# Token blocks 0 and 1 of the last matrix product joined to the seven-product groups, and the second gate's weight blocks converted inside the first gate

## The chip, the cores and the metric

The kernel runs on one core of one Trainium2 chip. The metric is the device time of one execution in microseconds (us), lower being better. The kernel before takes 741.22 us (median of 3 runs, 740.75 to 741.38).

## What is computed

The reference is a layer of two mixers on 2048 tokens of 1024 numbers. First `h = x + A(layernorm(x))`, where `A` is attention in four segments of 512 tokens with a memory that is carried from segment to segment. Then

```python
z  = gelu(layernorm(h) @ w_in)            # 2048 x 3584
z1 = z[:, :1792]
z2 = layernorm(z[:, 1792:])
g  = w_sp @ z2 + b_sp[:, None]            # w_sp is 2048 x 2048: over tokens
out = h + (z1 * g) @ w_out                # w_out is 1792 x 1024
```

The change is in the last two lines, but for one instruction that it moves in the attention part.

## The kernel before

Each engine has its own list of instructions, written out in program order by the Python code, and runs it in order. A recorder (`record`, line 87) derives the semaphore waits from the bytes that instructions read and write. Nothing is scheduled automatically: where a line stands in the code is where its instruction stands in its engine's queue. All instructions are issued through one helper, so that the profile gives them all line 214; they are told apart by their tiles. SyncE (SP in the profile) issues the DMAs.

**Attention.** A loop over n = 0 to 31 (segment and group of heads). In each pass TensorE makes projections, scores, products with values and, from the second segment on, eight-matmul pieces of the output projection (`ps<-wo,oT`); ScalarE makes the exponentials; VectorE normalises (`rd`, `otok`, `rdm`, `tm`), adds the residual (`hch`) and does parts of the next stage in between. One of these is `w_half` (line 932), which scales a 128x3584 piece of w_in from bfloat16 to float16 in one VectorE instruction (`wih<-win,sc`). `w_half(0)` stands at the end of pass 26 (line 1081) and `w_half(2)` at the end of pass 28.

**The gate** (`gate`, line 1257) is the product with w_sp. It runs twice: `gate(0, ...)` (line 1602) for output tokens 0 to 1023 and `gate(1, ...)` (line 1733) for tokens 1024 to 2047. Each half of w_sp is four blocks, b11, b12, b22 and b21, and four differences of them, t1 to t4 (`SUMS`, line 1236: t1 = b12 - b11, t2 = b22 - t1, t3 = b22 - b12, t4 = b21 - t2). With these, and with sums `ss` of z2's blocks (`s_sum`), a two-by-two block product takes seven block products, not eight. A gate has seven groups g of 128 + 128 channels, and a group is seven products of eight 128x512 matmuls: t2, t1, b11 or b21, t3, b21, t4, b22. ScalarE puts the bias into a PSUM bank before the first product adds to it (`seed_a`, `seed_b`, `seed_c`), and copies a bank out in the middle of a group (`copy_u`); VectorE takes results out (`out`) with the factor z1. After each product of a group the gate calls `each(g, k)`, k = 0 to 3, which places extra work there; `seam` is called after the first three b11 products.

The second gate's blocks are transposed early by DMA and parked in DRAM (`w_spT`). `q_load` (line 1219) brings one block back, 1 MB, `q_conv` (line 1222) scales it into float16 on VectorE (`b11g<-b11q,sc`, 128x4096), and `q_sum` makes one difference (128x4096). The g in a name marks the second gate's blocks and the h the first gate's (`b11h`). `HOME1` (line 424) gives each block its place in SBUF, which sets what must be dead before it can be loaded.

**Between the gates** stand four plain units (`units`, `out_unit`, lines 1519 and 1379): token blocks 0 and 1, times the two 512-wide halves of w_out, each 14 bfloat16 matmuls 128x512 (`ps<-w_out,z1T`), 56 in all. While TensorE runs them, VectorE makes t1, converts b22 and b21, and starts t2; b22 and b21 are loaded at that time too.

**The last product** is y = z1 * g times w_out. It runs for pairs of token blocks: two blocks, two halves of the contraction (seven chunks of 128 each) and two halves of the output make a two-by-two block product, and seven products of seven float16 matmuls do it (`NG = 7` groups, line 1672; `tcs` says which blocks; the loop at line 1770). These take y in float16 with a scale: the second gate writes it so (`z1x`); the first gate's results (`z1T`, bfloat16) are squared and summed on ScalarE (`y0_norm`) and converted on VectorE (`y0_conv`) during the second gate. VectorE also makes the sums of w_out's blocks (`ob_sum`) and of y's (`y_sum`) there.

Of the kernel before, what the change touches and what calls it, by code (L numbers as in the profile page):

```python
# [13 lines left out]
D = 1024  # L14
# [248 lines left out]
def bass_sequential_preLN__memory_aug_infini_attn__mixer_gmlp__prompt_kernel(  # L263
# [156 lines left out]
    WO1 = [tens("w_out1%d" % i, [128, 7, 512], BF16, o * K) for i, o in enumerate((14, 22))]  # L420
    WO0H = [tens("w_out0h%d" % i, [128, 7, 512], F16, o * K) for i, o in enumerate((54, 198))]
    STG = [tens("stg%d" % i, [128, 8, 128], BF16, o * K) for i, o in enumerate((54, 56, 58, 198, 200, 202))]
    WSPT = nc.dram_tensor("w_spT", (4, 128, 4, 1024), BF16, kind="Internal").ap()
    HOME1 = {"b11": 4, "b12": 118, "b22": 46, "b21": 126, "t1": 38, "t2": 22, "t3": 118, "t4": 14}
    RAW1 = {k: tens(k + "q", [128, 4, 8, 128], BF16, HOME1[k] * K) for k in ("b11", "b12", "b22", "b21")}
    BH1 = {k: tens(k + "g", [128, 4, 8, 128], F16, o * K) for k, o in HOME1.items()}
    SQ0 = tens("sq0", [128, 14], F32, 928)
# [3 lines left out]
    FIN2 = [tens("fin2%d" % i, [128, 2, 2, 512], BF16, o * K) for i, o in enumerate((4, 8, 22, 26))]  # L431
    OT4 = [[tens("ot%d%d" % (i, k), [128, 512], F32, (o + 2 * k) * K) for k in range(4)] for i, o in enumerate((38, 118))]
    SY = [tens("sy%d" % i, [128, 4, 7, 128], F16, o * K) for i, o in enumerate((14, 126))]
    FIN = [tens("fin%d" % i, [128, 512], BF16, o * K) for i, o in enumerate((21, 29, 13, 12))]

    PS = nc.alloc_psum_tensor("ps", [128, 8, 512], F32)
    R.space[PS[:, 0, :].tensor.name] = ("psum", 0)
# [12 lines left out]
    def next_bank(hold=False):  # L450
        if free:
            b = free.pop(0)
            if not hold:
                free.append(b)
            return b
        b = rot["banks"][rot["n"] % len(rot["banks"])]
        rot["n"] += 1
        return b

    def mm8(dst, lhs, rhs, n=8):  # L460
        for i in range(n):
            pe.matmul(dst, lhs(i), rhs(i), start=(i == 0), stop=(i == n - 1))
# [529 lines left out]
    for n in range(LAST + 1):  # L992
# [224 lines left out]
        sp.dma_start(WSPT[n // 4, :, n % 4, :], STG[n % 6][:].rearrange("p c n -> p (c n)"))  # L1217

    def q_load(k):
        sp.dma_start(RAW1[k][:].rearrange("p j c n -> p j (c n)"), WSPT[Q4.index(k)])  # L1220

    def q_conv(k):
        dve.tensor_single_scalar(BH1[k][:], RAW1[k][:], SC[0][:], ALU.mult)

    def q_sum(o):
        a, b = SUMS[o]
# [30 lines left out]
    def gate(pr, perm, seam=lambda: None, mid=lambda: None, each=lambda g, k: None):  # L1257
# [32 lines left out]
        def seed_a(g):  # L1290
            act.activation(bank(ba(g)), BROW[0][:], ACTF.Copy, scale=RINV[:])
# [10 lines left out]
        def p1(g):  # L1302
            prod(ba(g), a_blk(0, 0, g), "b11")
# [16 lines left out]
        for g in range(7):  # L1320
# [50 lines left out]
    fins = {}

    def fin_load(u, q=sp):
        tc, lo, w = u
        k = len(fins) % 4
        fins[u] = FIN[k]
        q.dma_start(FIN[k][:, 0:w], out2d[tc * 128:(tc + 1) * 128, lo:lo + w])

    def out_unit(u, wsl, q=sp):
        tc, lo, w = u  # L1380
        b = next_bank()
        mm8(PS[:, b, 0:w], lambda i: Z1T[:, i, tc * 128:(tc + 1) * 128], wsl, n=14)
        fin = fins[u]
        dve.tensor_tensor(fin[:, 0:w], fin[:, 0:w], PS[:, b, 0:w], ALU.add)
        q.dma_start(out2d[tc * 128:(tc + 1) * 128, lo:lo + w], fin[:, 0:w])
# [130 lines left out]

    w0_load(1)

    units = [(tc, 512 * h, 512) for h in range(2) for tc in range(2)]

    def seam():
        sp_half("b21")
        for k in range(1, 4):
# [19 lines left out]
    def total(n, src, o=TOT):  # L1543
        pool.tensor_copy(SQB[:, 0:n], src[:])
        pe.matmul(PS[:, 7, 0:n], ONES[:], SQB[:, 0:n], start=True, stop=True)
        dve.tensor_reduce(out=o[:], in_=PS[:, 7, 0:n], axis=mybir.AxisListType.X, op=ALU.add)
        dve.tensor_single_scalar(o[:], o[:], 1e-30, ALU.max)
# [15 lines left out]
        t = 1024 + 512 * k  # L1563
        sp.dma_start(BROW[k][:], B_b_sp[t:t + 512].partition_broadcast(128))

    def w1_load(i):
        sp.dma_start(WO1[i][:], wout[:, 7 * i:7 * i + 7, 512:D])

    def each0(g, k):
        z1_norm(g, k)  # L1570
        for h, lo in ((1, 14), (0, 22)):
            for n in range(14):
                if 4 * g + k == lo + n // 3:
                    w_norm(h, n)
            if 4 * g + k == lo + 4 and h:
                w0_load(0)
        if (g, k) == (0, 0):
            pool.tensor_single_scalar(TW[:], TOT[:], float(2 * T * FH), ALU.mult)
        if (g, k) == (5, 1):
            w1_load(0)  # L1580
            fin_load(units[0])
        if (g, k) == (4, 3):
            total(28, SQY, TOTY)
        if (g, k) == (6, 0):
            brow_in(1)
            q_load("b11")
            q_load("b12")
        if (g, k) == (6, 1):
            fin_load(units[1])
            w1_load(1)  # L1590
        if (g, k) == (6, 2):
            brow_in(0)
            fin_load(units[2])
            fin_load(units[3])
            q_conv("b11")
        if (g, k) == (6, 3):
# [5 lines left out]
    gate(0, banks, seam, mid, each0)  # L1602
    q_load("b22")
    q_load("b21")

    def brow_sq():
        for k in range(2):
            act.activation(bank(7), BROW[k][:], ACTF.Square, scale=float(np.sqrt(2.0)), accum_out=BSQ[:, k:k + 1])
# [4 lines left out]
        power(YS)  # L1613
        dve.tensor_tensor(INVY[:], INV[0][:], YS[:], ALU.mult)

    brow_sq()
    pool.tensor_tensor(TOT[:], TOTY[:], TW[:], ALU.mult)
    rot["banks"], rot["n"] = [banks[k] for k in (1, 2, 4, 6)], 0
    free.clear()
    q_sum("t1")  # L1620
    for n, u in enumerate(units):
        out_unit(u, (lambda i: WO0[i // 7][:, i % 7, :]) if u[1] == 0 else
                 (lambda i: WO1[i // 7][:, i % 7, :]))
        if n == 0:
            s_sum(1, 0)
            s_sum(2, 0)
        if n == 2:
            scale_y()
            q_conv("b21")
        if n == 1:  # L1630
            q_conv("b22")
    q_sum("t2")
    s_sum(3, 0)
    q_sum("t3")
    q_sum("t4")

    OBG = {"b12": 0, "b22": 2, "t1": 1, "t2": 3, "t3": 4, "t4": 5}
    OBW = {"b11": 0, "b21": 1}
# [16 lines left out]
        dve.tensor_tensor(ob_c(o, *r), ob_c(a, *r), ob_c(b, *r), ALU.subtract)  # L1655

    def y0_scale():
        total(14, SQ0)
# [12 lines left out]

    NG = 7

    def tcs(g):
        return (2 + g, 5 + g) if g < 3 else (5 + g, 9 + g)

    def y_blk(i, j, g):
        t = 128 * tcs(g)[i]
        return Z1X[:, 7 * j:7 * j + 7, t:t + 128]

    def sy(k, g):
        if g == 0:
            return Z1X[:, 7 * (k // 3):7 * (k // 3) + 7, 128 * (1 - k % 2):128 * (1 - k % 2) + 128]
        return SY[g % 2][:, k - 1]

    def y_sum(k, g):
# [16 lines left out]
    def job(g, k, f, *a):  # L1703
        jobs.setdefault((g, k), []).append((f, a))

    for r in range(14):
        job(*divmod(1 + r // 2, 4), y0_norm, r)
    for h in range(4):
        job(2 + (h + 1) // 4, (h + 1) % 4, y0_conv, h)
        job(3 + (h + 1) // 4, (h + 1) % 4, y_sum, h + 1, 0)  # L1710
    job(2, 0, y0_scale)
    job(0, 0, scale_w)
    for r in range(7):
        job(1, 0, ob_load, "b12", r)
# [14 lines left out]
        for f, a in jobs.get((g, k), ()):  # L1729
            f(*a)  # L1730

    perm1 = [banks[k] for k in (0, 3, 5, 1, 2, 4, 6)]
    gate(1, perm1, each=each1)

    def o_prod(b, a, w, first, lo=0, hi=512):
        for i in range(7):
# [103 lines left out]
```

## Time and profile before

| what | value |
|---|---|
| time, median of 3 runs | 741.22 us (740.75 to 741.38) |
| the profiled execution's own time | 741.11 us |
| its span, first to last instruction | 739.5 us |
| TensorE clock granted | 1.00 |
| VectorE busy | 579.5 us, 78% of the span |
| ScalarE busy | 478.0 us, 65% |
| GpSimd busy | 267.0 us, 36% |
| first gate's last stage before the plain units | ends at 565.72 us |
| plain units | 565.72 to 577.80 us |
| second gate | 577.80 to 662.46 us |
| last product, seven groups | 662.46 us to the end |

Times in the trace are microseconds from the span's start. In a line of the timeline come the start, the duration of the piece, the engine, the operation, the tile written and the tiles read, the shape, and how many instructions the piece holds; in brackets stands the idle time of the engine just before, and what ended it. PE is TensorE, DVE VectorE, ACT ScalarE, POOL GpSimd. A TensorE piece's duration has the drain of its last matmul in it, so that the pitch of the matmuls is read from the distance of starts.

### The profile page before, as it was taken

The page shows a single profiled execution, that of the slowest core. Times are in us where ns is not written, and L with a number is a line of the kernel's source. Part 1 is how long each engine was busy: PE and PEld are TensorE (multiplying, and loading weights), DVE is VectorE, ACT ScalarE, POOL GpSimd, SP SyncE. Part 2 cuts the span into 40 slices and gives each one's busy share as a digit, 9 for nine tenths or more (in the row PEclk, how much of TensorE's full clock was granted, in tenths as well). Part 3 has the DMA queues.
Part 4 walks back from the last instruction along what each step waited for, and adds up shares of the span by engine and source line. Part 5 has one row for each costly group of instructions (what it writes and reads, how often), then busy time and mean ns, then how long its engine had stood idle before and what let it go on. Part 6 is the DMA issues. An engine that isn't in the chain of part 4 may idle for free.

```text
span 739.5 us, 13541 instructions
## 1 busy us (share of the span) xinstructions
PE 733.4 (99%) x5399; PEld 351.7 (48%) x5399; DVE 579.5 (78%) x1027; ACT 478.0 (65%) x684; POOL 267.0 (36%) x423
## 2 busy tenths in 40 slices
PE   8999999999999999999999999999999999999998
PEld 4444544544555445545554444444444444444444
DVE  5578889889988989878896777874556778866676
ACT  6777888888887888826886669966866282210000
POOL 2565555545554333110153899600000100005342
PEclk9999999999999999999999999999999999999999
DMA  9656568466645752654050036399539211031311
GB/s 302 176 172 149 114 149 180 126 155 161 172 101 165 250 178 59 169 131 129 29 142 1 1 58 128 60 198 188 168 123 329 68 44 35 1 114 64 107 58 57
DMA packets 148798, 92.64 MB, mean 125 GB/s; under 512 B 105984, under 2 KB 132864, under 8 KB 148224
## 3 DMA queue, kind: packets, MB, share of 16 engines
q1 hardware_dynamic: 147920, 91.00, 46.9%
q8 instruction: 42, 0.69, 0.4%
q10 hardware_dynamic: 816, 0.79, 0.3%
q14 instruction: 20, 0.16, 0.1%
HBM read 56.11 MB, written 12.58 MB: 93 GB/s over the span
## 4 chain that ended last, share of the span: by engine, by line
PE 96%; DVE 3%; DMA 1%; issue 0%; ACT 0%; DVEq 0%
PE ps L214 96%; DVE sq L214 1%; DMA wv<-in_A_wv_dram 1%; DVE hch L214 0%; DVE ps L214 0%; DVE otok L214 0%; DVE rd L214 0%; DVE wih L214 0%; DVE stats L214 0%; ACT L214 0%; DVE rdm L214 0%; DVE pqk L214 0%; DVE fin L214 0%; DVEq L224 0%; DVE tot L214 0%
## 5 line engine op out<-in xcount | busy, mean ns | idle before, releaser
L214 ACT ACTIVATE e<-ps 128x2048 bf16<-128x2048 f32 (+1 forms) x96 | 152.6, 1590 | 21.2 <-PE ps L214 20.5
L214 POOL TENSOR_SCALAR_AFFINE_SELECT e<-e 128x512 bf16<-128x512 bf16 x128 | 83.9, 669 | 127.1 <-ACT e L214 127.1
L214 PE MATMUL ps<-xnT,wk 128*128 128x512 bf16 x256 | 60.8, 380 | 0.2 <-DVE hch L214 0.2
L214 PE MATMUL ps<-wv,xnT 128*128 128x512 bf16 x256 | 59.7, 380 | 0.9 <-DMA wv<-in_A_wv_dram 0.6
L214 PE MATMUL ps<-xnT,wq 128*128 128x512 bf16 x256 | 60.5, 379 | 0.0
L214 POOL TENSOR_TENSOR ot<-ot,fin 128x512 f32<-128x512 f32 x21 | 27.8, 1351 | 86.5 <-ACT ot L214 86.5
L214 PE MATMUL ps<-wo,oT 128*128 128x512 bf16 x256 | 58.2, 380 | 0.0
L214 PEld LDWEIGHTS ps<-v,e 128*128 128x128 bf16 x1280 | 38.8, 96 | 14.0 <-issue 6.5
L214 ACT ACTIVATE ot<-ps,invo 128x512 f32<-128x512 f32 x7 | 4.8, 687 | 60.8 <-PE ps L214 60.8
L214 PE MATMUL ps<-v,e 128*128 128x33 bf16 x1280 | 42.2, 178 | 0.0
L214 DVE BATCH_NORM_STATS2 zst<-z 128x6 f32<-128x448 bf16 x64 | 38.1, 610 | 0.0
L214 POOL TENSOR_TENSOR sz<-wzh 128x512 f16<-128x512 f16 x28 | 33.7, 1206 | 11.4 <-PE ps L214 11.3
L214 ACT ACTIVATE tmp_u<-ps,invy 128x512 f32<-128x512 f32 x14 | 9.6, 688 | 43.5 <-PE ps L214 43.5
L214 PE MATMUL ps<-z2h,sy 128*128 128x512 f16 (+2 forms) x182 | 37.4, 363 | 0.0
L214 PEld LDWEIGHTS ps<-wo,oT 128*128 128x128 bf16 x256 | 23.9, 98 | 27.8 <-DVE hch L214 0.5
L214 PEld LDWEIGHTS ps<-xnT,wk 128*128 128x128 bf16 x256 | 22.6, 98 | 30.2 <-issue 5.7
L214 ACT ACTIVATE qk<-ps 128x512 bf16<-128x512 f32 x48 | 28.7, 599 | 12.7 <-PE ps L214 12.7
L214 PEld LDWEIGHTS ps<-wv,xnT 128*128 128x128 bf16 x256 | 23.2, 98 | 27.8 <-DMA wv<-in_A_wv_dram 1.3
L214 DVE TENSOR_TENSOR zt<-ps,zt 128x512 f32<-128x512 f32 x28 | 19.1, 686 | 20.4 <-PE ps L214 15.9
L214 PE MATMUL ps<-qk 32*128 32x128 bf16 (+3 forms) x512 | 34.5, 302 | 0.6 <-DVE tm L214 0.6
L214 PEld LDWEIGHTS ps<-xnT,wq 128*128 128x128 bf16 x256 | 23.5, 98 | 22.9 <-issue 0.2
L214 ACT ACTIVATE ps<-ps 128x512 f32<-128x512 f32 (+1 forms) x42 | 23.8, 568 | 13.9 <-PE ps L214 13.9
(281 smaller groups left out, 1668.6 us busy)
## 6 DMA issues: line engine op xcount, KB each, us to landing
nb<-in_B_w_in_dram SPq DMA_DIRECT2D x16, 448.0 KB, 4.1
nb<-in_B_w_sp_dram SPq DMA_DIRECT2D x14, 512.0 KB, 4.6
w_out<-in_B_w_out_dram SPq DMA_DIRECT2D x6, 896.0 KB, 5.7
xch<-in_A_x_dram SPq DMA_DIRECT2D x16, 256.0 KB, 4.5
xr<-in_A_x_dram SPq DMA_DIRECT2D x16, 256.0 KB, 4.1
out_dram<-hch SPq DMA_DIRECT2D x16, 256.0 KB, 2.4
w_spT<-stg SPq DMA_DIRECT2D x16, 256.0 KB, 4.0
out_dram<-fin SPq DMA_DIRECT2D x31, 128.0 KB, 1.7
```

Source lines behind the costliest of these rows:

```text
L214: ins = getattr(e, op.name)(*op.args, **op.kw)
```

## The change

- The four plain units go, with their loads of w_out's second half and of the residual. `NG` becomes 8 and `tcs` starts at blocks 0 and 4: all sixteen token blocks run in eight groups of seven products.
- The second gate's blocks get other places, so that they can be loaded and converted while the first gate still runs. Each load is two DMAs of 512 KB. VectorE converts b11, b12 and half of b22; ScalarE converts the other half of b22 in two instructions, and b21 in four (`q_part`, 128x1024 each). t1 is made inside the first gate's last group, and t2, t3 and t4 after the second gate's first three products (`seam1`).
- The bias rows are loaded at the first gate's (4, 0) and their norm taken at (5, 0); the second gate's scale is computed at (5, 2).
- `y0_norm` takes 28 squares of 512, into a PSUM bank, one pair in each stage from (0, 1) to (3, 2). `y0_conv` becomes eight ScalarE instructions of 128x1792 from (4, 1) to (6, 0); the first group's `y_sum` calls move to (5, 2) to (6, 2).
- In the attention part `w_half(0)` moves from the end of pass 26 to the end of pass 27.

```diff
-    HOME1 = {"b11": 4, "b12": 118, "b22": 46, "b21": 126, "t1": 38, "t2": 22, "t3": 118, "t4": 14}
+    HOME1 = {"b11": 14, "b12": 4, "b22": 118, "b21": 22, "t1": 126, "t2": 38, "t3": 4, "t4": 46}
...
         if n == 26:
             scale_end(1)
+        if n == 27:
             w_half(0)
...
     def q_load(k):
-        sp.dma_start(RAW1[k][:].rearrange("p j c n -> p j (c n)"), WSPT[Q4.index(k)])
-
-    def q_conv(k):
-        dve.tensor_single_scalar(BH1[k][:], RAW1[k][:], SC[0][:], ALU.mult)
+        for j in (0, 2):
+            sp.dma_start(RAW1[k][:, j:j + 2].rearrange("p j c n -> p j (c n)"), WSPT[Q4.index(k)][:, j:j + 2])
+
+    def q_conv(k, lo=0):
+        dve.tensor_single_scalar(BH1[k][:, lo:4], RAW1[k][:, lo:4], SC[0][:], ALU.mult)
+
+    def q_part(k, n):
+        act.activation(BH1[k][:, n], RAW1[k][:, n], ACTF.Copy, scale=SC[0][:])
...
         for g in range(2 * (pr == 0), 3):
             seed_a(g)
+        if pr:
+            q_part("b22", 0)
+            q_part("b22", 1)
         p1(0)
...
+        if (g, k) == (4, 0):
+            brow_in(1)
+            brow_in(0)
         if (g, k) == (4, 3):
             total(28, SQY, TOTY)
+        if (g, k) == (5, 0):
+            brow_sq()
+            pool.tensor_tensor(TOT[:], TOTY[:], TW[:], ALU.mult)
+        if (g, k) == (5, 1):
+            q_load("b11")
+        if (g, k) == (5, 2):
+            scale_y()
         if (g, k) == (6, 0):
-            brow_in(1)
-            q_load("b11")
             q_load("b12")
+            q_load("b22")
         if (g, k) == (6, 1):
+            q_load("b21")
+            q_conv("b11")
+            s_sum(1, 0)
         if (g, k) == (6, 2):
-            q_conv("b11")
+            s_sum(2, 0)
             q_conv("b12")
+            q_sum("t1")
...
-    for n, u in enumerate(units):
-        out_unit(u, (lambda i: WO0[i // 7][:, i % 7, :]) if u[1] == 0 else
-                 (lambda i: WO1[i // 7][:, i % 7, :]))
...
+    def seam1():
+        q_conv("b22", 2)
+        q_sum("t2")
+        for n in range(4):
+            q_part("b21", n)
+        s_sum(3, 0)
+        q_sum("t3")
+        q_sum("t4")
...
     def y0_norm(r):
-        act.activation(Z1T[:, 0:3, 0:256], Z1T[:, r, 256:1024].rearrange("p (a n) -> p a n", n=256), ACTF.Square,
-                       accum_out=SQ0[:, r:r + 1])
+        for h in range(2):
+            act.activation(bank(7), Z1T[:, r, 512 * h:512 * h + 512], ACTF.Square,
+                           accum_out=SQ0[:, 2 * r + h:2 * r + h + 1])
 
     def y0_conv(n):
-        for h in range(2):
-            s = (slice(None), slice(7 * (n // 2), 7 * (n // 2) + 7), slice(256 + 384 * (n % 2) + 192 * h, 448 + 384 * (n % 2) + 192 * h))
-            dve.tensor_single_scalar(Z1X[s], Z1T[s], YS0[:], ALU.mult)
-
-    NG = 7
+        q, r = (0, 2, 1, 3)[n // 2], 7 * (n % 2)
+        s = (slice(None), slice(r, r + 7), slice(256 * q, 256 * q + 256))
+        act.activation(Z1X[s], Z1T[s], ACTF.Copy, scale=YS0[:])
+
+    NG = 8
 
     def tcs(g):
-        return (2 + g, 5 + g) if g < 3 else (5 + g, 9 + g)
+        return (g, g + 4) if g < 4 else (4 + g, 8 + g)
...
     for r in range(14):
-        job(*divmod(1 + r // 2, 4), y0_norm, r)
+        job(*divmod(1 + r, 4), y0_norm, r)
+    job(4, 0, y0_scale)
+    for n in range(8):
+        job(*divmod(17 + n, 4), y0_conv, n)
     for h in range(4):
-        job(2 + (h + 1) // 4, (h + 1) % 4, y0_conv, h)
-        job(3 + (h + 1) // 4, (h + 1) % 4, y_sum, h + 1, 0)
-    job(2, 0, y0_scale)
+        job(*((5, 2), (5, 3), (6, 1), (6, 2))[h], y_sum, h + 1, 0)
...
-    perm1 = [banks[k] for k in (0, 3, 5, 1, 2, 4, 6)]
-    gate(1, perm1, each=each1)
+    perm1 = [banks[k] for k in (1, 2, 4, 0, 3, 6, 5)]
+    gate(1, perm1, seam1, each=each1)
```

More of the change, by code (lines that the diff above doesn't have):

```diff
@@ L419, in bass_sequential_preLN__memory_aug_infini_attn__mixer_gmlp__prompt_kernel @@
     WO0 = [tens("w_out0%d" % i, [128, 7, 512], BF16, o * K) for i, o in enumerate((54, 198))]
-    WO1 = [tens("w_out1%d" % i, [128, 7, 512], BF16, o * K) for i, o in enumerate((14, 22))]
     WO0H = [tens("w_out0h%d" % i, [128, 7, 512], F16, o * K) for i, o in enumerate((54, 198))]
@@ L423, in bass_sequential_preLN__memory_aug_infini_attn__mixer_gmlp__prompt_kernel @@
     WSPT = nc.dram_tensor("w_spT", (4, 128, 4, 1024), BF16, kind="Internal").ap()
-    HOME1 = {"b11": 4, "b12": 118, "b22": 46, "b21": 126, "t1": 38, "t2": 22, "t3": 118, "t4": 14}
+    HOME1 = {"b11": 14, "b12": 4, "b22": 118, "b21": 22, "t1": 126, "t2": 38, "t3": 4, "t4": 46}
     RAW1 = {k: tens(k + "q", [128, 4, 8, 128], BF16, HOME1[k] * K) for k in ("b11", "b12", "b22", "b21")}
     BH1 = {k: tens(k + "g", [128, 4, 8, 128], F16, o * K) for k, o in HOME1.items()}
-    SQ0 = tens("sq0", [128, 14], F32, 928)
+    SQ0 = tens("sq0", [128, 28], F32, 768)
     SQW = b3("sqw", [128, 28], F32)
@@ L430, in bass_sequential_preLN__memory_aug_infini_attn__mixer_gmlp__prompt_kernel @@
     TOTY = tens("toty", [128, 1], F32, 992)
-    FIN2 = [tens("fin2%d" % i, [128, 2, 2, 512], BF16, o * K) for i, o in enumerate((4, 8, 22, 26))]
-    OT4 = [[tens("ot%d%d" % (i, k), [128, 512], F32, (o + 2 * k) * K) for k in range(4)] for i, o in enumerate((38, 118))]
+    FIN2 = [tens("fin2%d" % i, [128, 2, 2, 512], BF16, o * K) for i, o in enumerate((38, 42, 4, 8))]
+    OT4 = [[tens("ot%d%d" % (i, k), [128, 512], F32, (o + 2 * k) * K) for k in range(4)] for i, o in enumerate((22, 118))]
     SY = [tens("sy%d" % i, [128, 4, 7, 128], F16, o * K) for i, o in enumerate((14, 126))]
-    FIN = [tens("fin%d" % i, [128, 512], BF16, o * K) for i, o in enumerate((21, 29, 13, 12))]
     PS = nc.alloc_psum_tensor("ps", [128, 8, 512], F32)
@@ L1369, in gate @@
             each(g, 3)
[L1371 to L1385, printed above, removed]
     def brow_load(pr, q=sp):
@@ L1517, in bass_sequential_preLN__memory_aug_infini_attn__mixer_gmlp__prompt_kernel @@
     w0_load(1)
-    units = [(tc, 512 * h, 512) for h in range(2) for tc in range(2)]
     def seam():
@@ L1564, in brow_in @@
         sp.dma_start(BROW[k][:], B_b_sp[t:t + 512].partition_broadcast(128))
-    def w1_load(i):
-        sp.dma_start(WO1[i][:], wout[:, 7 * i:7 * i + 7, 512:D])
     def each0(g, k):
@@ L1578, in each0 @@
             pool.tensor_single_scalar(TW[:], TOT[:], float(2 * T * FH), ALU.mult)
-        if (g, k) == (5, 1):
-            w1_load(0)
-            fin_load(units[0])
+        if (g, k) == (4, 0):
+            brow_in(1)
+            brow_in(0)
         if (g, k) == (4, 3):
             total(28, SQY, TOTY)
+        if (g, k) == (5, 0):
[5 more added lines that the diff above has]
+            scale_y()
         if (g, k) == (6, 0):
-            brow_in(1)
-            q_load("b11")
             q_load("b12")
+            q_load("b22")
         if (g, k) == (6, 1):
-            fin_load(units[1])
-            w1_load(1)
+            q_load("b21")
+            q_conv("b11")
+            s_sum(1, 0)
         if (g, k) == (6, 2):
-            brow_in(0)
-            fin_load(units[2])
-            fin_load(units[3])
-            q_conv("b11")
-        if (g, k) == (6, 3):
+            s_sum(2, 0)
             q_conv("b12")
+            q_sum("t1")
     assert full >= set(range(7)), full
@@ L1601, in bass_sequential_preLN__memory_aug_infini_attn__mixer_gmlp__prompt_kernel @@
     assert sorted(banks) == list(range(7)) and banks[:2] == pre, (free, pre)
-    gate(0, banks, seam, mid, each0)
-    q_load("b22")
-    q_load("b21")
     def brow_sq():
@@ L1614, in scale_y @@
         dve.tensor_tensor(INVY[:], INV[0][:], YS[:], ALU.mult)
-    brow_sq()
-    pool.tensor_tensor(TOT[:], TOTY[:], TW[:], ALU.mult)
-    rot["banks"], rot["n"] = [banks[k] for k in (1, 2, 4, 6)], 0
+    gate(0, banks, seam, mid, each0)
     free.clear()
-    q_sum("t1")
-    for n, u in enumerate(units):
-        out_unit(u, (lambda i: WO0[i // 7][:, i % 7, :]) if u[1] == 0 else
-                 (lambda i: WO1[i // 7][:, i % 7, :]))
[L1624 to L1635, printed above, removed]
+    def seam1():
[6 more added lines that the diff above has]
+        q_sum("t4")
     OBG = {"b12": 0, "b22": 2, "t1": 1, "t2": 3, "t3": 4, "t4": 5}
@@ L1657, in y0_scale @@
     def y0_scale():
-        total(14, SQ0)
+        total(28, SQ0)
         power(YS0)
@@ L1681, in sy @@
     def sy(k, g):
-        if g == 0:
-            return Z1X[:, 7 * (k // 3):7 * (k // 3) + 7, 128 * (1 - k % 2):128 * (1 - k % 2) + 128]
         return SY[g % 2][:, k - 1]
@@ L1740, in iv @@
     def iv(g):
-        return (INVO0 if g < 3 else INVO)[:]
+        return (INVO0 if g < 4 else INVO)[:]
     obank = [perm1[k] for k in (1, 2, 0, 4, 3, 6, 5)]
```

## The prediction

> **What bounds the kernel now.** First the page's busy times and its chain of work that ended last:
>
> ```profile
> PE 733.4 (99%) x5399; PEld 351.7 (48%) x5399; DVE 579.5 (78%) x1027; ACT 478.0 (65%) x684; POOL 267.0 (36%) x423
> ...
> PE 96%; DVE 3%; DMA 1%; issue 0%; ACT 0%; DVEq 0%
> ```
>
> TensorE (PE) is on the path for 96% of the span, so a matmul taken away is worth its pitch, and other engines count only where the chain leaves PE. The chain in order of time shows where that is:
>
> ```profile
> 9.38 239.32 PE ps L214 x2633
> ...
> 263.22 1.32 DVE wih L214
> ...
> 267.53 0.69 DVE hch L214
> 268.21 0.05 issue
> 268.26 48.76 PE ps L214 x517
> 317.02 0.03 issue
> 317.04 419.27 PE ps L214 x1998
> ```
>
> After the start it leaves PE once, from 248.7 to 268.3 us (passes 25 and 26 of the attention), where VectorE (DVE) carries it, with `w_half(0)` (the row `wih`, 1.32 us) in the middle. PE's timeline there:
>
> ```profile
> 258.14 1.90 PE L214 MATMUL ps<-xnT,wk 128*128 128x512 bf16 x8
> ...
> 267.67 0.39 PE L214 MATMUL ps<-qk 32*128 32x512 bf16 x4 [0.59 <-DVE tm L214]
> 268.26 1.90 PE L214 MATMUL ps<-xnT,wk 128*128 128x512 bf16 x8 [0.20 <-DVE hch L214]
> 277.45 1.90 PE L214 MATMUL ps<-xnT,wk 128*128 128x512 bf16 x8
> ```
>
> Pass to pass, from wk product to wk product, the starts are 10.12 us apart over pass 26 and 9.19 over the next. So pass 26 loses 0.93 us, and PE's two waits there are for DVE's `tm` and `hch`, both queued behind `wih`. Last, the seam between the gates:
>
> ```profile
> 563.99 1.89 PE L214 MATMUL ps<-b22h,ss 128*128 128x512 f16 x8
> 565.72 12.25 PE L214 MATMUL ps<-w_out,z1T 128*128 128x512 bf16 x56
> 577.80 5.34 PE L214 MATMUL ps<-b11g,z2h 128*128 128x512 f16 x24
> 582.99 1.89 PE L214 MATMUL ps<-t1g,ss 128*128 128x512 f16 x8
> 584.71 1.89 PE L214 MATMUL ps<-t2g,ss 128*128 128x512 f16 x8
> 586.44 1.89 PE L214 MATMUL ps<-b21g,z2h 128*128 128x512 f16 x8
> ```
>
> No wait stands in brackets: PE runs through. The 56 plain matmuls hold PE for 577.80 - 565.72 = 12.08 us, 215.8 ns each, and that is also the time in which DVE makes t1, converts b22 and b21, and in which both are loaded.
>
> **Step 1, the matmuls.** 56 go and a group of 7 x 7 = 49 comes. In the last product a group starts every 10.57 us (668.50, 679.08, 689.66), 215.8 ns a matmul again. So 12.08 - 10.57 = **1.51 us less**. The Trainium skill, "TensorE: Matmul & The Clock Gate", section "Back-to-back issue gap", gives both N / 2.4 + 2.5 ns, which is 215.8 ns for 512 columns, and a sustained 131 ns; by the second the seven matmuls would be worth 0.92 us. Every stretch of 128x512 matmuls quoted here has the first.
>
> **Step 2, w_half(0).** Without it in pass 26, DVE reaches `tm` 1.33 us sooner (263.13 to 264.46 is its slot), ending at 266.28, and `hch` at 266.88. PE without the stall starts the scores at 266.9 and the wk product at 268.26 - 0.93 = 267.33. Both are then ready, so the whole 0.93 us goes. In pass 27 the instruction stands between `mv` and `rd`; there DVE now idles 1.35 us (273.55 to 274.90, waiting for ScalarE's `e`), which takes 1.33 us just so, and `tm` (ended 276.08) has another 1.0 us until PE's scores at 277.12. `w_half(2)` stands at the same place in pass 28 now, and PE has no wait there. If that cover were gone, the stall would come back one pass later. Bounds 0 and 0.93, I take **0.93 us less**, since pass 28 is the same case without a stall.
>
> **Step 3, the seam without its cover.** PE now goes from the last b22 product at 565.72 straight to b11 (to 570.90), t1 (to 572.62), t2 (to 574.36), b21, t3 at 576.1, b21, t4 at 579.5. Who is late?
>
> *DMA.* The loads wait for a dead block and leave SP as these products end: b11 at 552.1, b12 at 557.3, b22 at 559.0, b21 at 560.7. In the kernel before, the same loads took 4.8, 6.9, 7.0 and 9.1 us from issue to landing, the last with other loads in flight. At up to those, b11 is there at 557.0, b12 at 564.2, b22 at 566.0, b21 at 569.8. SP has nothing else queued there, as the other loads are gone.
>
> *DVE.* It idles from 557.37 to 561.46 now; b11's conversion (1.28) and one `ss` (0.69) go in there. Then, by start-to-start distances of the same rows: `vb` and `z1T` from 561.46 to 562.59, `out` 0.66, `ss` 0.60, b12 from 563.85 (1.28; a late landing at 564.2 moves it by 0.35), t1 (2.29) to 567.4, three results (0.66 + 1.13) to 569.2, half of b22 (0.75, as the 128x2048 `w_out0h` row), t2 from 569.95 to **572.2**; PE wants it at 572.62, so 0.4 us is left. Then `ss`, t3 to 575.0 (wanted 576.1) and t4 to 577.3 (wanted 579.5).
>
> *ScalarE (ACT).* Its queue is full until 565.05 with the w_out squares. Then three seeds, six conversions and two more seeds:
>
> ```profile
> L214 ACT ACTIVATE b22h<-b22r,sc 128x1024 f16<-128x1024 bf16 x4 | 4.6, 1145 | 0.0
> ```
>
> That is the price of a conversion, 1.145 us; back to back they start some 0.08 sooner than a full duration (three bias seeds of 0.679 span 1.90 us), say 1.06. Seeds at 564.95, 565.56, 566.17; the first ends at 565.63 against PE's start at 565.72: nothing, or 0.1 us. b22's two parts 566.8 to 568.9, seeds b and c to 570.1 (PE's t1 wants the bank at 570.90), b21's four parts 570.0 to **574.4**. PE wants b21 at 574.36 to 574.5: no slack at all. At 1.06 each the stall is 0 to 0.1, at a full 1.145 each it is 0.5. The Trainium skill, "ScalarE: Activation LUTs", section "What ACT_TABLE_LOAD costs", has 186 ns + 0.833 ns an element, 93 ns for a scale operand, and 93 ns of overlap back to back: 1.13 us and a pitch of 1.04. By it the stall is 0; the row agrees on the duration, and no run before has six in a row.
>
> I take **0.2 us more** for the two places together (bounds 0 and 0.6).
>
> *What else is added there.* The squares of the bias rows (2 x 0.79 us) fall at 548.2 into an ACT gap of 2.2 us. The scale of the second gate needs GpSimd's short chain (about 2 to 3 us after 549.7) and stands in DVE's queue at 552.9, before a result that PE frees at 553.8: hidden.
>
> **Step 4, inside the second gate.** DVE loses the eight y conversions (4.5 us) and is idle more. ACT gets 14 pairs of squares (2 x 0.79 in each stage): between `copy_u` 3 of one group and `copy_u` 2 of the next it needs three stages, 4.7 us, of 6.9. The y conversions (128x1792, float16 out, scale from memory) are not in the trace; 128x1792 squares take 1.70 and the scale adds about 0.1 by the 1024 rows (1.049 and 1.145), so 1.8 (1.7 to 1.95). The tightest place is group 5: from 649.4 three of them end at 654.6, `copy_u` 2 of group 6 ends at 655.2, and PE's t3 needs the bank at 655.55. Left 0.35; **0** taken, at 1.95 each 0.1. The sum of squares and its scale (`y0_scale`) moves from group 2 to 4 with its 2 us on DVE; DVE's idle of 1.0 us at 644.4 and 2.5 at 655.7 take it up, and nothing PE waits for comes near.
>
> **Sum.** 741.11 (the profiled execution; its span of 739.5 and 1.6 around it) - 1.51 - 0.93 + 0.2 = 738.87. The median is 0.11 above the profiled time, so **738.9 us**, 0.31% less.
>
> **Rivals.**
> 1. *w_half(0) only moves its stall* (12%): its slot grows or `e` is late, and pass 27 loses what 26 gained. For it: the idle it fills is exactly its size. Against: 1.0 us more of slack behind, and pass 28. The time: 738.9 + 0.93 = 739.8, not to be told from no change.
> 2. *ScalarE paces the seam* (14%): its six parts come at full duration or wait for each other, b21 is 0.5 to 1.2 us late, t4 and the results follow. For it: zero slack. Time 739.2 to 739.9, about 739.5.
> 3. *The loads are late, and the kernel is slower* (6%). Place: ACT, waiting for b22's first half at 566.8 with two seeds and b21's parts queued behind. With no slack at b21, each microsecond later than 566.8 is one of PE. It passes the time before once b22 lands after 566.8 + 2.24 = 569.0, that is 10.0 us after issue, and by over 0.2% after 570.5. For it: 3 MB are issued within 3.4 us, and the busiest load before took 9.1. Against: that was with w_out and residual loads in flight, and b22's first half is the third and fourth of eight pieces. At a landing of 571.5 the time is 743.6.
>
> **How the numbers follow.** The forecast has 68%, the rivals 12, 14 and 6. Range: low end with no stall at all (738.7) less 0.3 for the spread of the runs shown (740.75 to 741.38), 738.4; the high end takes in rivals 1 and 2, and both halfway, 740.1. About 0.2% (1.48 us, 739.74) is what a measurement can tell from no change. Faster than that: 68 of the forecast and 9 of rival 2 = 77%; within: 12 + 5 and 1 of rival 3 = 18%; slower: 5%.
>
> **What would show it.** PE's matmuls fall by 7 and the last product lasts eight times 10.57 us. Pass 26 takes 9.2 us from wk to wk and pass 27 still 9.2. At the seam PE's waits name ACT (bank or `b21g`), 0.3 us or less; a wait for `t2g` on DVE, or ACT waiting for a DMA, shows rival 2 or 3. The prediction is wrong if PE waits more than 0.6 us at the seam, in pass 27, or at group 5's end.

## The result and the profile after

The changed kernel takes 739.67 us (median of 22 runs, 738.97 to 741.58), the kernel before 741.25 us beside it (22 runs, 740.27 to 743.25): 1.58 us less, a ratio of 0.9980 [0.9974, 0.9986]. The profiled execution took 739.93 us, its span 738.1. The forecast was 738.9 us, a gain of 2.3; two thirds of that came. One execution, the profiled one of the repeat e0_again below, took 1247.95 us at a granted clock of 0.56; it is left out, and e0_again has no profile.

The page of the changed kernel, busy times and the shares of the chain that ended last:

```profile
PE 728.5 (99%) x5328; PEld 350.8 (48%) x5392; DVE 578.6 (78%) x1024; ACT 504.7 (68%) x727; POOL 268.5 (36%) x426
...
PE 94%; DVE 3%; DMA 1%; issue 1%; ACT 0%; POOL 0%; ACTq 0%; DVEq 0%
```

TensorE is still the bound. The weight loads (PEld) are 5392, seven fewer than before, while of the matmuls themselves some records are missing. What is to be explained lies in single waits. PE's timeline in passes 26 and 27:

```profile
258.84 1.90 PE L214 MATMUL ps<-xnT,wk 128*128 128x512 bf16 x7
...
267.70 0.39 PE L214 MATMUL ps<-qk 32*128 32x512 bf16 x4
268.02 1.90 PE L214 MATMUL ps<-xnT,wk 128*128 128x512 bf16 x7
...
277.21 1.90 PE L214 MATMUL ps<-xnT,wk 128*128 128x512 bf16 x7
```

From wk product to wk product it is 9.18 and 9.19 us, where pass 26 took 10.12: both waits are gone, and no new one stands in pass 27. VectorE there has `w_half(0)` between `mv` and `rd`:

```profile
270.87 1.10 DVE L214 TENSOR_SCALAR wih<-win,sc 128x3584 f16<-128x3584 bf16 x1
271.89 0.25 DVE L214 RECIPROCAL rd<-ps 128x16 f32<-128x16 f32 x1
...
274.66 0.17 DVE L214 TENSOR_SCALAR rdm<-ps 128x16 f32<-128x16 f32 x1 [0.85 <-ACT e L214]
```

It takes 1.02 us of the queue here, not the 1.33 it took in pass 26, and 0.85 us of the idle time for `e` is left: the cover was wider than the forecast had it. The last product, at the starts of the 28 matmuls of each group, still takes 10.57 to 10.58 us a group:

```profile
660.97 6.21 PE L214 MATMUL ps<-z2h,sy 128*128 128x512 f16 x28
...
671.55 6.21 PE L214 MATMUL ps<-z2h,sy 128*128 128x512 f16 x28
...
682.12 6.21 PE L214 MATMUL ps<-z2h,sy 128*128 128x512 f16 x28
```

At the seam, first PE, then ScalarE:

```profile
563.77 1.89 PE L214 MATMUL ps<-b22h,ss 128*128 128x512 f16 x8
565.49 5.34 PE L214 MATMUL ps<-b11g,z2h 128*128 128x512 f16 x24
570.67 1.89 PE L214 MATMUL ps<-t1g,ss 128*128 128x512 f16 x8
572.40 1.89 PE L214 MATMUL ps<-t2g,ss 128*128 128x512 f16 x8
574.13 1.89 PE L214 MATMUL ps<-b21g,z2h 128*128 128x512 f16 x8
...
577.61 1.89 PE L214 MATMUL ps<-b21g,z2h 128*128 128x512 f16 x8
579.33 1.89 PE L214 MATMUL ps<-t4g,z2h 128*128 128x512 f16 x8
```

```profile
564.73 1.90 ACT L214 ACTIVATE ps<-brow,rinv 128x512 f32<-128x512 bf16 x3
566.57 2.17 ACT L214 ACTIVATE b22g<-b22q,sc 128x1024 f16<-128x1024 bf16 x2
...
569.78 4.25 ACT L214 ACTIVATE b21g<-b21q,sc 128x1024 f16<-128x1024 bf16 x4
```

Every product starts 1.72 to 1.73 us after the one before (5.18 after the 24): the seam costs nothing here. ScalarE's last b21 conversion ends at 574.03 and PE's b21 product starts at 574.13, so the slack is as small as the forecast had it. Four conversions take 4.25 us, a pitch (from start to start) of 1.03 us, (4.25 - 1.145) / 3.

One new wait is in group 4 of the second gate. PE there, and then VectorE:

```profile
625.98 1.89 PE L214 MATMUL ps<-t4g,z2h 128*128 128x512 f16 x8
627.94 1.90 PE L214 MATMUL ps<-b22g,ss 128*128 128x512 f16 x8
```

```profile
624.03 0.18 DVE L214 TENSOR_REDUCE tot<-ps 128x1 f32<-128x28 f32 x1
...
625.07 0.15 DVE L214 TENSOR_SCALAR top<-top 128x1 int32<-128x1 int32 x1 [0.67 <-POOL top L214]
...
625.89 0.16 DVE L214 RECIPROCAL invo<-invo 128x1 f32<-128x1 f32 x1
626.00 0.62 DVE L214 TENSOR_SCALAR z2h<-z,scw 128x1536 f16<-128x1536 bf16 x1
626.53 0.68 DVE L214 TENSOR_TENSOR z2h<-z2h 128x1024 f16<-128x1024 f16 x1
627.14 0.74 DVE L214 SCALAR_TENSOR_TENSOR vb<-ps,invy,tmp_u 128x512 bf16<-128x512 f32 x1
```

From t4g to b22g it is 1.96 us, not 1.73: 0.23 us lost. `vb` takes a result out of the bank to which the b22 product adds next (`out(g, 1, t2, bc(g), ...)` ahead of `prod(bc(g), SS[:, 3], "b22")` in `gate`). It ends at 627.88 and stands behind the chain of `y0_scale` (624.03 to 626.0, with 0.67 us of waiting for GpSimd in it), one piece of w_out's scaling and one of its sums.

**Where the time went**, profile against profile (741.11 and 739.93 us, -1.18):

| part | us |
|---|---|
| matmuls (12.08 - 10.57) | -1.51 |
| pass 26 (10.12 - 9.18) | -0.94 |
| seam | 0 |
| wait for b22g, group 4 | +0.23 |
| start: first wk product at 14.44, not 13.74 us | +0.70 |
| own time less span: 1.88, not 1.58 us | +0.30 |
| sum | -1.22 |

(All wk products from the first to that of pass 26 are 0.69 or 0.70 us later than in the profile before.) The wait, the start and the time outside the span are in no step of the forecast. What the last two are, and why the timed runs gain 1.6 and not 2.2, is what most of the experiments are for.

### The profile page after: what moved, and what is told of

Same layout as the page of the kernel before. It is cut to its first block, busy times and chain, and to the rows that moved or that the text cites. A ratio compares the mean times of both kernels' runs of the same rounds, so it can differ in the third digit from the quotient of the medians.

```text
span 738.1 us, 13506 instructions
## 1 busy us (share of the span) xinstructions
PE 728.5 (99%) x5328; PEld 350.8 (48%) x5392; DVE 578.6 (78%) x1024; ACT 504.7 (68%) x727; POOL 268.5 (36%) x426
## 4 chain that ended last, share of the span: by engine, by line
PE 94%; DVE 3%; DMA 1%; issue 1%; ACT 0%; POOL 0%; ACTq 0%; DVEq 0%
PE ps L214 94%; DMA wv<-in_A_wv_dram 1%; DVE stats L214 1%; DVE lno L214 0%; DVE hch L214 0%; DVE pqk L214 0%; DVE ps L214 0%; DVE ss L214 0%; DVE otok L214 0%; DVE z2h L214 0%; ACT e L214 0%; DVE etmp L214 0%; DVE rd L214 0%; ACT L214 0%; DVE vb L214 0%
## 5 line engine op out<-in xcount | busy, mean ns | idle before, releaser
L214 POOL TENSOR_TENSOR ot<-ot,fin 128x512 f32<-128x512 f32 x24 | 31.9, 1355 | 69.5 <-ACT ot L214 69.5
L214 PE MATMUL ps<-xnT,wq 128*128 128x512 bf16 x226 | 54.0, 379 | 1.6
L214 PE MATMUL ps<-z2h,sy 128*128 128x512 f16 (+2 forms) x238 | 49.9, 366 | 0.0
L214 PEld LDWEIGHTS ps<-z2h,sy 128*128 128x128 f16 x238 | 22.7, 98 | 26.0 <-DVE ot L214 0.3
L214 ACT ACTIVATE ps<-z1T 128x512 f32<-128x512 bf16 x56 | 33.5, 598 | 1.3
```

The source lines that it names most:

```text
L214: ins = getattr(e, op.name)(*op.args, **op.kw)
```

## The experiments

The theory after the first look: the two gains are as forecast, `y0_scale` costs 0.23 us, and the rest is an early or late start by chance. The rival: the seam, without a wait in this one profile, loses time in others. The table has all runs; "b12" is the time from the issue of its second half to its landing, "seam" what PE loses from b11g to t4g, "start" the offset of PE against the first profile of the kernel before, all from that run's profile. e0 to e4 and e6 to e8 ran on one chip, the others on a second and a third; for the first row no chip is on record. The seam's losses of e4 and e5 are in the main made by their edits; e6 moves where PE waits.

| run | median us | less than before beside it | ratio, interval | b12 | seam | start |
|---|---|---|---|---|---|---|
| changed kernel | 739.67 | 1.58 | 0.9980 [0.9974, 0.9986] | 5.2 | 0 | 0.70 |
| e0_again (10 executions) | 739.74 | 1.55 | 0.9985 [0.9976, 0.9994] | - | - | - |
| e1_whalf_only | 740.31 | 0.98 | 0.9985 [0.9976, 0.9994] | - | - | 0.57 |
| e2_whalf_back | 740.57 | 0.72 | 0.9990 [0.9981, 0.9999] | 6.8 | under 0.1 | -0.04 |
| e3_y0_early | 739.44 | 1.85 | 0.9977 [0.9968, 0.9986] | 7.0 | 0.24 | 0.18 |
| e4_dve_all | 740.97 | 0.33 | 0.9998 [0.9989, 1.0007] | 7.6 | 2.5 | 0.0 |
| e6_seam_cut | 739.73 | 1.57 | 0.9978 [0.9969, 0.9987] | 7.4 | 0.6 | 1.6 |
| e7_before_again | 741.32 | -0.02 | 1.0003 [0.9994, 1.0012] | - | - | 2.4 |
| e8_late_half | 739.26 | 2.04 | 0.9975 [0.9967, 0.9984] | 6.2 | 0 | 0.13 |
| (second chip) e10_after_profile | 738.98 | 2.08 | 0.9975 [0.9965, 0.9985] | 5.3 | 0 | 0.60 |
| e9_split_b12 | 738.57 | 2.49 | 0.9965 [0.9954, 0.9976] | 5.4 | 0 | -0.3 |
| e5_act_b22 | 741.40 | -0.34 | 1.0007 [0.9999, 1.0016] | 5.1 | 2.0 | 0.0 |
| (third chip) e11_few_squares | 739.32 | 2.09 | 0.9973 [0.9961, 0.9984] | 7.6 | 0.26 | 0.1 |

An interval of 0.1% is 0.7 us, so differences of single kernels below that are read from the traces. The column of gains is of medians. The means of the same executions give less for the changed kernel, 1.46 us in the first row, 1.19 in e0_again and 1.91 in e10_after_profile; for e1 they give 1.00 and for e2 0.76.

### The two gains by themselves

e0_again is the changed kernel, for comparison.

> The changed kernel once more, unaltered. In the first trace of it three things differ from the kernel before on TensorE: the start (the first wk product 0.65 us later, behind a DMA of wv), pass 26 of the attention (0.89 us sooner), and the last product and the seam (1.51 us sooner, 0.23 us lost in group 4 of the second gate). Theory: the start is chance, so the kernel is 2.1 to 2.2 us faster than the one before and the start of this trace need not be late (first wk product anywhere from 13.7 to 14.5 us). Rival: the late start belongs to the changed program, then the start is late again and the kernel is 1.4 to 1.6 us faster.

The gain, 1.55 us by medians, is the rival's figure; the theory's 2.1 to 2.2 was missed. That does not make the rival right: without a profile of this run the start can't be seen, and the time outside the span, found below, lowers the theory's figure by 0.3. (By the rows above, the start is 0.70 us later and pass 26 gains 0.94, where this text has 0.65 and 0.89.)

e1_whalf_only is the kernel before with one line more:

```diff
         if n == 26:
             scale_end(1)
+        if n == 27:
             w_half(0)
```

> The kernel before with one line of the change: w_half(0) moved from the end of pass 26 to the end of pass 27. Theory: the stall of pass 26 goes whole and does not come back, 0.9 us faster than the kernel before; wk to wk 9.2 us in pass 26 and in pass 27. Rival: the stall moves to pass 27, time as before. If the late start belongs to the whole change, the start here is as in the kernel before.

It gains 0.98 us. In its trace the wk products start at 258.71, 267.89 and 277.08 us: 9.18 and 9.19 again. Step 2 is right, by trace and by time.

e2_whalf_back is the changed kernel with `w_half(0)` back in pass 26.

```diff
         if n == 26:
             scale_end(1)
-        if n == 27:
             w_half(0)
```

> The changed kernel with w_half(0) put back to pass 26. Theory: pass 26 loses 0.9 us again, so 1.2 to 1.3 us faster than the kernel before by matmul count and group 4 alone (1.51 - 0.23). Rival: the move was worth nothing, then the time is that of the changed kernel.

It is 0.83 us above e0_again by medians and 0.43 by means; in its trace pass 26 takes 10.13 us again. It gains 0.72 us on the kernel before. That is less than the 1.28 that the matmuls and group 4 leave; the 0.30 outside the span accounts for half of what is missing, and the rest is within the interval.

### The wait in group 4

```diff
-    job(4, 0, y0_scale)
+    job(3, 3, y0_scale)
```

> The changed kernel with the sum of squares and scale for y (y0_scale) called at the end of group 3 of the second gate, not in stage 0 of group 4. Theory: in the changed kernel VectorE's read of the bank (vb of group 4) stands behind that 2 us chain and TensorE's b22 product of group 4 waits 0.23 us for it; earlier, the read is done 1.7 us sooner, the wait goes, 0.2 us faster than the changed kernel, and the second gate runs at 1.727 us a product throughout. Rival: the chain now makes something in group 3 or 4 late, no gain.

The time is 739.44, 0.30 below e0_again, a difference too small to be told from chance by the times. In its trace the wait is gone; here PE in group 4, then at the seam, then VectorE ahead of t1:

```profile
625.72 1.89 PE L214 MATMUL ps<-t4g,z2h 128*128 128x512 f16 x8
627.44 1.89 PE L214 MATMUL ps<-b22g,ss 128*128 128x512 f16 x8
```

```profile
570.17 1.89 PE L214 MATMUL ps<-t1g,ss 128*128 128x512 f16 x8
572.06 1.90 PE L214 MATMUL ps<-t2g,ss 128*128 128x512 f16 x8
...
577.28 1.89 PE L214 MATMUL ps<-b21g,z2h 128*128 128x512 f16 x8
579.06 1.90 PE L214 MATMUL ps<-t4g,z2h 128*128 128x512 f16 x8
```

```profile
562.53 0.68 DVE L214 TENSOR_TENSOR ss<-ss,z2h 128x1024 f16<-128x1024 f16 x1
563.62 1.29 DVE L214 TENSOR_SCALAR b12g<-b12q,sc 128x4096 f16<-128x4096 bf16 x1 [0.41 <-DMA b12q<-w_spT]
```

Group 4 runs at 1.72 us. But t2g starts 1.89 us after t1g and t4g 1.78 after b21g: this execution loses 0.24 us at the seam. Here b12's second half landed 7.0 us after its issue, and VectorE stood idle 0.41 us for it with t1 and t2 behind. In the changed kernel's profile it took 5.2 us, with code up to there that is the same. So the seam's loss is not settled by one profile.

### Who sets the seam

e4_dve_all: VectorE converts all of b22 and b21.

```diff
-        if pr:
-            q_part("b22", 0)
-            q_part("b22", 1)
...
-        q_conv("b22", 2)
+        q_conv("b22")
         q_sum("t2")
-        for n in range(4):
-            q_part("b21", n)
+        q_conv("b21")
```

> The changed kernel with all of b22 and b21 converted by VectorE (two instructions 128x4096) and none by ScalarE. Theory: the seam is paced by the engines that convert; VectorE then carries 0.75 + 1.3 us more ahead of t2 and t3. TensorE waits 0.2 us for t2g, 0.5 for t3g and about 0.2 at the first b22 product, 0.9 us in all: 740.6 by the changed kernel's 739.7. Rival: the landing of b12 and b21 paces the seam, whoever converts: within 0.25 of the changed kernel, and TensorE's waits at the seam below 0.2 us.

It takes 740.97, 1.2 us above e0_again: the rival falls. The theory had 0.9 us, and this profile loses 2.5 us from b11g to t4g. PE waits 1.09 us there for t2g, where 0.2 was expected; VectorE had stood idle 0.97 us for b12, which landed after 7.6 us. VectorE, then PE:

```profile
564.02 1.29 DVE L214 TENSOR_SCALAR b12g<-b12q,sc 128x4096 f16<-128x4096 bf16 x1 [0.97 <-DMA b12q<-w_spT]
```

```profile
573.00 1.90 PE L214 MATMUL ps<-t2g,ss 128*128 128x512 f16 x8 [1.09 <-DVE t2g L214]
...
577.09 1.89 PE L214 MATMUL ps<-t3g,ss 128*128 128x512 f16 x8 [0.45 <-DVE t3g L214]
...
581.19 1.90 PE L214 MATMUL ps<-t4g,z2h 128*128 128x512 f16 x8 [0.49 <-ACT tmp_u L214]
```

e5_act_b22: ScalarE converts all of b22.

```diff
             q_part("b22", 0)
             q_part("b22", 1)
+            q_part("b22", 2)
+            q_part("b22", 3)
...
-        q_conv("b22", 2)
```

> The changed kernel with all four quarters of b22 converted by ScalarE, none by VectorE. Theory (ScalarE has no slack at the seam, one conversion is 1.05 us of its queue): its two further conversions stand ahead of the bias for t1's bank and of b21's four. TensorE's t1 waits about 1.3 us for the bank and its b21 product another 0.7 for b21g: 2.1 us in all, 741.8. Rival (VectorE's chain over t1, t2, t3 and t4 sets the seam, and ScalarE's conversions stand beside it): VectorE gains 0.75 us, TensorE waits at most 0.5, 739.5 to 740.2.

741.40 us, 2.4 above e10_after_profile on the same chip. PE at its seam:

```profile
571.23 1.90 PE L214 MATMUL ps<-t1g,ss 128*128 128x512 f16 x8 [1.13 <-ACT ps L214]
...
575.42 1.90 PE L214 MATMUL ps<-b21g,z2h 128*128 128x512 f16 x8 [0.57 <-ACT b21g L214]
```

Counted from b11g, t1g comes 1.29 us later than in the changed kernel's trace and b21g 0.73 more, 2.02 in all where 2.1 was expected. ScalarE has no slack: two conversions more cost PE their whole price, twice the pitch of 1.03 us. The Trainium skill, "ScalarE: Activation LUTs", section "What ACT_TABLE_LOAD costs", has the figures for an estimate of the pitch of such a conversion, 186 ns + 0.833 ns x 1024 + 93 ns for the scale operand - 93 ns of overlap, which is 1.04 us; the four b22 parts here take 4.25 us, and it agrees.

e6_seam_cut makes PE independent of the late blocks in the second gate's first group, by letting it read b11g for all of them, which leaves the right weights out of that part of the output.

```diff
-        def prod(b, a, w):
+        def prod(b, a, w, cut=False):
+            if pr and cut:
+                w = "b11"
...
-            prod(ba(g), a_blk(0, 1, g), "b21")
+            prod(ba(g), a_blk(0, 1, g), "b21", g < 2)
...
-            prod(bb(g), SS[:, 1], "t2")
+            prod(bb(g), SS[:, 1], "t2", not g)
...
```

The products with t1, t3, t4 and b22 get the same `not g`.

> The changed kernel, but in the first group of the second gate every product reads the block b11g in place of t1g, t2g, b21g, t3g, t4g and b22g (and the b21 product of the second group too), so that TensorE waits for no late block at the seam; loads, conversions and differences are made as before, and that part of the output is another. The trace parts of the changed kernel give 741.1 - 1.51 - 0.91 + 0.23 = 738.9, but it is timed at 739.7 to 739.8. Theory: the missing 0.8 us is not lost at the seam, where its profile shows no wait of TensorE. Then this kernel is timed within 0.25 of the changed one (739.5 to 740.0). Rival: in most executions, other than the profiled one, the loads of b12, b22 and b21 land later, and the seam loses 0.4 to 0.8 us. Then this kernel is timed at 739.0 to 739.3. The group-4 wait for b22g of 0.2 us stays by both.

739.73 us, as the theory had it, but it does not tell the two apart. PE's waits for the blocks are gone, yet VectorE still makes them late (0.81 us for b12, landed after 7.4 us), its results behind them come late, ScalarE's bias and copy wait for those, and PE waits one step further on:

```profile
580.84 1.90 PE L214 MATMUL ps<-b11g,z2h 128*128 128x512 f16 x8 [0.45 <-ACT tmp_u L214]
```

The lateness travels along three engines' queues; cutting PE's reads doesn't cut it.

e8_late_half is e3 with less traffic behind b12:

```diff
-            q_load("b22")
+            q_load("b22", (0,))
...
-            q_load("b21")
+            q_load("b21", (0,))
+            q_load("b22", (2,))
+            q_load("b21", (2,))
```

> The kernel with y0_scale one stage earlier (e3), and the second half of b22 loaded after the first half of b21, not ahead of it, so that b12 has 0.5 MB less beside it on its way. Theory: b12 came late in e3 (second half 7.0 us after issue, VectorE waits 0.41 us for it, TensorE 0.24 at the seam) because the whole of b22 was issued 1.7 us behind it. Then b12's second half lands within 5.5 us, VectorE waits under 0.1 us for it and TensorE at the seam under 0.1; time 739.2, that is 0.2 below e3 and 0.5 below the changed kernel. Rival: b12's landing varies by itself (3.7 to 7.0 us seen) whatever is issued behind it: it lands at 5 to 7 us again and TensorE loses 0.1 to 0.3 at the seam, 739.4.

PE loses nothing at its seam and the time is 739.26, as the theory wanted; but its reason is not shown. b12's second half took 6.2 us, not the 5.5 or less of the theory, inside the 5.1 to 7.6 seen with the old order. Why it varies stays open: in the four profiles of this chip with the old order it took 6.8 to 7.6 us, in the three of the second chip 5.1 to 5.4, in the one of the third 7.6.

e10_after_profile is the changed kernel once more, on that second chip.

> The changed kernel, unaltered, for a second profile. Theory: b12's second half lands 6 to 7.6 us after issue, not 5.2; VectorE waits 0.1 to 1 us for it ahead of b12g, and TensorE 0.1 to 0.6 us at the seam (for t2g, or for ScalarE's tmp_u ahead of t4g); the wait for b22g in group 4 is 0.2 again. Time 739.6 to 739.9. Rival: the profile shows no wait at the seam again, and the landing is 5.2 us or less; then late landings belong to the other kernels.

Here the rival was right: b12 landed after 5.3 us, and no product at the seam is late, in both profiles of the changed kernel. It gains 2.08 us, against 1.55 on the first chip. e9_split_b12, beside it, is e3 with VectorE's conversion of b12 in two, the first half in idle time ahead of `vb`:

```diff
             q_conv("b11")
             s_sum(1, 0)
+            q_conv("b12", 0, 2)
...
-            q_conv("b12")
+            q_conv("b12", 2)
```

> The kernel with y0_scale one stage earlier (e3), and VectorE's conversion of b12 in two instructions: the first half stands ahead of vb in the last group, where VectorE idles 1.6 to 1.8 us, the second half where the whole stood. b12's second half landed 5.2 us after its issue in the changed kernel's profile, and 6.2 to 7.6 us in five others; VectorE wants it after 6.5 us. Theory: this landing is what the seam loses by, 0.1 to 0.5 us in most executions. With 0.55 us less to do after the landing, t1g starts at most 0.8 us after it, TensorE waits under 0.1 us at the seam, and the time is 738.9 to 739.2, 0.3 to 0.5 below e3's 739.4 and 0.6 to 0.9 below the changed kernel. Rival: the seam loses nothing in most executions, late landings or not, since the slack of 0.4 us at t2g covers them; then the time is that of e3, 739.3 to 739.5.

```profile
559.27 0.75 DVE L214 TENSOR_SCALAR b12g<-b12q,sc 128x2048 f16<-128x2048 bf16 x1 [0.77 <-DMA b12q<-w_spT]
...
562.64 0.75 DVE L214 TENSOR_SCALAR b12g<-b12q,sc 128x2048 f16<-128x2048 bf16 x1
```

It is the fastest, 738.57 us, a ratio of 0.9965 [0.9954, 0.9976], and 0.41 below the changed kernel beside it, of which 0.23 is group 4. As b12 landed early for all three kernels of that chip, the split could not show its worth there. On the third chip, in e11, b12 took 7.6 us and the split kernel still lost 0.26 us (t2g 0.20, t4g 0.06): it moves the limit, and not far enough.

### The start, and the time outside the span

> The kernel before, unaltered, as a second profile and a measure of what two equal kernels differ by. Both theories: a ratio of 1.000 with an interval of about 0.001 on each side. Theory: the start (first weight load of TensorE to the first wk product) varies by execution by 0 to 0.7 us, in the kernel before as in the changed one, since their first 240 us hold the same instructions; a second profile of the kernel before starts 0.2 to 0.6 us later than the first. Rival: the late start belongs to the changed kernels; the second profile starts within 0.1 us of the first.

The two are equal in time, and the second profile of the kernel before starts 2.4 us late: the theory holds, the size was far off. PE at the start of that execution, and the windows of the first microseconds of it (after the five engines' busy times stand the granted clock, the DMA share and GB/s):

```profile
6.80 0.62 PE L214 MATMUL ps<-ident,lno 128*128 128x128 bf16 x8 [0.19 <-DVE lno L214]
8.77 3.28 PE L214 MATMUL ps<-wv,xnT 128*128 128x512 bf16 x8 [1.35 <-DMA wv<-in_A_wv_dram]
```

```profile
8.00:10.00 2.00, 1.23 (x4) 0.52 (x5) 0.57 (x2) 1.94 (x5) 0.00 (x0) 0.78 1.13 346
10.00:12.00 2.00, 2.00 (x7) 0.77 (x6) 1.21 (x3) 1.16 (x2) 0.68 (x2) 0.50 1.20 287
```

The load of wv came late, PE waited 1.35 us (0.57 in the first profile), and then the clock was granted at 0.50, so that eight matmuls took 3.28 us in place of 2.11. The starts in the table, from -0.3 to 2.4 us in programs with the same first 240 us, follow neither the kernel nor the chip. The changed kernel's two are alike, 0.70 and 0.60, but the kernel before has 0 and 2.4, and e3, with the same instructions up to there, 0.18. So nothing ties the 0.70 to the change, and I take it as chance.

The 0.30 outside the span is not chance. Own time less span is 1.55 to 1.58 us as a mean of every set of runs of the kernel before and of e1, and 1.85 to 1.89 in every kernel with eight groups (the changed kernel: 1.866 over 22 runs, standard error 0.005). After the span's end the instruction queue brings one block of 8 KB in the first kind (0.6 us after it), and two in the second (0.6 to 0.9 and 1.3 to 1.5 us after). ScalarE had grown by 41 instructions, so e11_few_squares takes 42 away from e9:

```diff
-        for h in range(2):
-            act.activation(bank(7), Z1T[:, r, 512 * h:512 * h + 512], ACTF.Square,
-                           accum_out=SQ0[:, 2 * r + h:2 * r + h + 1])
+        act.activation(bank(7), Z1T[:, r, 0:512], ACTF.Square, scale=2.0, accum_out=SQ0[:, r // 2:r // 2 + 1])
...
-    for r in range(14):
+    for r in range(0, 14, 2):
         job(*divmod(1 + r, 4), y0_norm, r)
```

> The kernel with b12 in two conversions (e9), and 7 of the 28 squares that the scale of the first gate's results is made from (one of 512 tokens in every second chunk, each weighted by four), so that ScalarE has 42 instructions less: 737 in the trace, one below the kernel before, against 779. It leaves out three quarters of the sum that this scale is taken from. The time around the span (own time less span) is 1.57 us in the kernel before in all its executions, and 1.85 to 1.88 in every kernel with eight groups; after their span the instruction queue brings two blocks of 8 KB, in the kernel before one. Theory: the second block belongs to ScalarE, whose instructions grew by 41 past the end of a block. Then one block is left after the span, the time around it is 1.57, and the span, in which TensorE waited for none of the squares, is that of e9: 0.28 us below e9, a ratio to the kernel before of about 0.9962. Rival: the block belongs to another engine or has nothing to do with it; two blocks remain and the time around the span is 1.85 again.

Two blocks remain (0.6 and 1.3 us after the span), and the time around the span is 1.859: my theory falls. The block isn't ScalarE's, or has nothing to do with it. GpSimd's list grew too, from 423 to 426 instructions on the two pages, and no run varies that. Which engine's list is meant, and whether the second block makes the 0.29 us or only comes with it, stays open. The Trainium skill, "Runtime: NRT & Kernel Launch", section "Instruction fetch mechanics", says that each engine fetches its next block of instructions by itself while it executes, mostly hidden, in blocks of 16 KiB; the trace has such blocks in one queue and 8 KB in another, and no run here shows what a block costs at the end.

## Why the prediction was right in sign and short in size

- **Step 1, the matmuls:** right. A group takes 10.57 us in the eight groups as in the seven; -1.51 in the sum of the traces.
- **Step 2, w_half(0):** right, 0.94 by trace (0.93 taken) and 0.98 by e1's time. `w_half(0)` takes 1.02 us of the queue in pass 27, not 1.33, so it did not fill the idle time "just so". Rival 1, the stall moved by one pass, is shown wrong by the 9.19 us of pass 27.
- **Step 3, the seam:** the 0.2 us was put at the wrong place, and in the changed kernel's own two profiles the seam costs nothing. ScalarE had no slack, and its pitch came at 1.03 us (1.06 taken), so it cost nothing (rival 2 did not happen, though e5 shows how near it was). What is late, where something is, is b12's second half in VectorE's queue: I had it landing 6.9 us after issue, moving t1 by 0.35 inside a slack of 0.4 us. It lands after 5.1 to 7.6 us, and where it came late in kernels with the seam's work dealt out as in the changed kernel (e2, e3, e11) PE lost 0 to 0.26 us. Rival 3 had the right mechanism at the wrong block, b22, and far too long.
- **Step 4, inside the second gate:** one part of this step failed. "The sum of squares and its scale (`y0_scale`) moves from group 2 to 4 with its 2 us on DVE; DVE's idle of 1.0 us at 644.4 and 2.5 at 655.7 take it up, and nothing PE waits for comes near." In group 4 `vb` comes behind it, and PE waits for `vb` by way of the bank. I had looked for the readers of the scale, not for what queues behind it. It costs 0.23 us; e3 takes it away. The rest of the step was right: `y0_conv` takes 1.78 us (taken: 1.8) and `copy_u` 2 of group 6 ends at 642.99, ahead of t3 at 643.49.
- **The sum** took the 1.6 us around the span as fixed. They became 1.87: 0.29 us that no step had, the same in every kernel with eight groups.

With these, -1.51 - 0.94 + 0.23 + 0.29 is -1.93, and 0 to 0.26 more at the seam gives -1.67 to -1.93. The timed gains are 1.58, 1.55 and 2.08 by medians. The last, on the chip where b12 landed early, is 0.15 more than the sum allows, and the first chip's is 0.12 less (0.48 less by means), all inside their intervals; so the times bear the sum out only to about half a microsecond. The difference between the chips, 0.53 us, fits the landings, but is within what the intervals leave to chance, no run changed the landing alone, and there is no profile of the changed kernel that is known to be from the first chip. The forecast came as near as it did in part by luck: the 0.2 us at the seam, which did not come where it was put, made up for part of the 0.52 us that no step had.

## What to carry to other kernels

Before a chain of small instructions is moved in a queue, look at the next instruction behind it that frees a bank or a buffer for the bound engine, not only at who reads the chain's result. A load that lands just in time is to be costed by its landings over several executions and chips: the changed kernel's profile showed 5.2 us, others up to 7.6. And where the gain hoped for is below 1 us, compare own time and span apart: the time outside the span can change with the program.

## What was not expected of the hardware

- The start varies by 2.7 us between executions of the same instructions: in the latest, 1.35 us of waiting for a load, and then a stretch at a granted clock of 0.50, where 128x512 matmuls came 0.43 us apart. The Trainium skill, "TensorE: Matmul & The Clock Gate", section "Part 1: The HAM clock gate", has a half clock after about 3.4 us of idleness; here it followed a wait of 1.35 us, so this trace does not fit that figure by itself. No run here varies that wait alone.
- The time outside the span differs by 0.29 us between programs, and by no more than 0.04 between sets of runs of the same kind.
- The same 512 KB load, in the same place of the same instructions, landed 5.1 to 5.4 us after issue on one chip (three profiles), and 6.8 to 7.6 on two others (four profiles and one). From 557 to 562 us of the changed kernel's profile, with b12 and the first of b22 and b21 on their way, the DMA moved 160 to 340 GB/s; from 563 to 566 us, with b22 and b21 alone, about 400.
